# Which hidden pairs stay in plain f32, where VectorE adds up an accumulator, and at which steps the side jobs of the next batch start, in a fused attention and feed-forward kernel

## The chip, the cores and the metric

The kernel runs on one core of one Trainium2 chip. The metric is the device time of one execution in microseconds. Before the change it was 2100.04 us, the median of three runs (2099.92 to 2102.28). The profiled execution took 2101.02 us, and its span, from the first instruction to the last, is 2099.2 us.

## The reference

Four batches of 12480 tokens with 128 channels go through an attention with 49 agents and then through a feed-forward layer with 2048 hidden units. Everything is f32.

```python
a2k = sm(agents, k)            # softmax over the 12480 keys, scaled by 1/sqrt(128)
agent_v = a2k @ v              # 49 x 128 per batch
q2a = sm(q, agents)            # softmax over the 49 agents
x = (q2a @ agent_v).reshape(49920, 128)
h = x @ w_in                   # 49920 x 2048
g = h - np.tanh(h)
return g @ w_out
```

## The kernel before

The kernel never builds `x`. For each batch it multiplies the 49 agent values by `w_in` once (`project`), so that a hidden value is the product of a token's 49 softmax weights with a 49 x 2048 matrix, kept as a high part `awh` and a low part `awl` in float32r.

The main loop (`fast`, line 820 on) goes over 100 blocks of up to 500 tokens. A block has 8 steps, and a step works on one pair of hidden chunks, 2 x 128 hidden units. Two blocks make a **round** of 16 steps; `pos`, 0 to 15, is the step's place in the round. The text numbers steps by this position. There are 50 rounds. In one step:

- TensorE does the first layer of the step two ahead (`m1`, line 559): six float32r matmuls into a two-bank PSUM buffer `h`.
- ScalarE makes `y = tanh(h)` (line 569) and `z`, a scaled square of `y` (line 574). The cubic law `h - tanh(h)` is near `h * z` for small values.
- VectorE makes the product `g = h * z` (line 579), which also frees the buffer `h`.
- For a **split pair** GpSimd rounds `g` to float32r, the high part `gh` (line 609), and VectorE subtracts it, which gives the low part `gl` (line 614), one step later and behind the next product. TensorE then does the second layer (`m2`, line 628) with twelve float32r matmuls: high part by low and high weights, low part by high weights.
- For a **plain pair** there is no `gh` and no `gl`. TensorE multiplies `g` itself in f32 (`acc<-g,wo_f`). The table `PLAIN` on line 61 names the positions of plain pairs; the first block of all is plain throughout.

The second layer of step k-1 stands on TensorE in step k, behind the first layer of step k+2. It adds up over 8 steps in a two-bank accumulator `acc`. PSUM holds four such two-bank buffers in all, for `h`, `acc`, the transposes `pt` and the side jobs' `misc`. When a block is done, ScalarE copies the first bank out (`take`, line 640) and VectorE adds the second bank to it (`add_up`, line 637), which frees the accumulator. That is at positions 2 and 10, two steps into the next block.

Each round also makes the softmax weights of the next round's tokens: 64 small matmuls (line 504) at about position 4, five short VectorE instructions (lines 517 to 523) between the products of positions 8 and 9, and two transposes at 11 and 15. Beside the first three batches run the side jobs for the next batch (`phase1`): 13 score jobs, the maximum, 13 value jobs (`av`: a subtraction on GpSimd, line 342; an exponential on ScalarE, line 346; 8 matmuls, line 354; an addition to an SBUF sum on VectorE, line 366), the sum and four projection parts (`project`). The tables `KS`, `VS`, `OS` on lines 72 to 75 say at which positions how many jobs of each kind start, and `VGAPS` how many steps a value job rests before its exponential and before its matmuls. A round holds three score jobs, or three value jobs, or neither.

The order of all instructions on each engine is the order in which this Python code issues them (`issue_order`). In a step: the product, then the copy-out and addition of a finished accumulator, then the running side jobs, then tanh and square of the next step, the first layer, the low part, the second layer, and last the starts of new side jobs.

Of the kernel before, what the change touches and what calls it, by code (L numbers as in the profile page):

```python
# [57 lines left out]
LATE = 3  # L58
KV = 3
VB = 4  # L60
PLAIN = (1, 3, 5, 7, 9, 13)
NB = dict(y=2, z=2, g=4, gh=3, gl=3)
Q0 = 2
NV = 10
# [5 lines left out]
T0 = 11  # L70
T1 = 15
KS = {2: 1, 12: 2}
VS = {5: 1, 9: 1, 13: 1}
VGAPS = {5: (6, 2), 9: (3, 1), 13: (4, 2)}
OS = {2: 1, 10: 1}


def width(n):
# [23 lines left out]
class Build:  # L102
# [116 lines left out]
    def phase1(self, b):  # L219
        nc = self.nc  # L220
        st = {}
        kb, vb = (K0 if b == 0 else KV), VB
# [27 lines left out]
        def ahead(kind, load, g, depth):  # L250
            have = st.setdefault(kind, [])
            while len(have) < min(NG, g + depth):
                have.append(load(len(have)))
            return have[g]
# [77 lines left out]
            st["mb_at"] = self.last_name()  # L332

        def av(g, gaps=(0, 1)):
            vt = ahead("v", load_v, g, vb - 1) if b else None
            n = tiles(g)
            sv = st["s"][:, g * GT * A : (g * GT + n) * A].rearrange("p (t a) -> p t a", a=A)
            e3 = sv
            flat = e3.rearrange("p t a -> p (t a)")
            top = st["mb"][:, None, :].broadcast_to([128, n, A])  # L340
            first = self.count()
            (nc.gpsimd if b else nc.vector).tensor_tensor(e3, sv, top, ALU.subtract)
            if b:
                self.wait_for(first, self.mul_at)
            yield from (None,) * (gaps[0] if b else 1)
            nc.scalar.activation(e3, e3, AF.Exp, scale=SCALE)
            yield from (None,) * gaps[1]
            if b:
                ps = self.misc()
                for t in range(n):  # L350
                    r = rows(g, t)
                    odd = t % 2
                    w = A if odd else HALF
                    nc.tensor.matmul(  # L354
                        ps[HALF * odd : HALF * odd + w, : C + 1],
                        flat[:r, t * A : t * A + w],
                        vt[:r, t, : C + 1],
                        start=t < 2,
                        stop=t >= n - 2,
                    )  # L360
                yield
                acc = st["acc"][: HALF + A]
                if g == 0:
                    nc.vector.tensor_copy(acc, ps[: HALF + A, : C + 1])
                else:
                    nc.vector.tensor_tensor(acc, acc, ps[: HALF + A, : C + 1], ALU.add)
                return
            vt = ahead("v", load_v, g, 1)
            if g == 0:
                ph = self.banks("h")  # L370
                st["ps"], st["pr"] = ph[:, 0, :], ph[:, 1, :A]
            ps = st["ps"]
            for t in range(n):
                r = rows(g, t)
                odd = t % 2
                w = A if odd else HALF
                nc.tensor.matmul(
                    ps[HALF * odd : HALF * odd + w, :C],
                    flat[:r, t * A : t * A + w],
                    vt[:r, t, :C],  # L380
                    start=(g == 0 and t < 2),
                    stop=(g == NG - 1 and t >= n - 2),
                )
            yield
            if g == NG - 1:
                em = st["em"]
                for i, (rhs, r) in enumerate(((em, 128), (e3[:, 0, :], 128), (e3[:, 1, :], TAIL))):
                    nc.tensor.matmul(st["pr"], self.ones[:r, :], rhs[:r], start=(i == 0), stop=(i == 2))
                return
            if g in (0, 1):  # L390
                return
            if g in (2, 3):
                st["es", g % 2] = self.work.tile([128, GT * A], F32, tag="es", name="es", bufs=2)
            es = st["es", g % 2]
            e0 = st["s"][:, (g - 2) * GT * A : (g - 1) * GT * A] if g in (2, 3) else es
            nc.vector.tensor_tensor(es, e0, flat, ALU.add)
            if g == NG - 2:
                es = st["es", 0]
                nc.vector.tensor_tensor(es, es, st["es", 1], ALU.add)
                st["em"] = self.small.tile([128, A], F32, tag="m", name="es")  # L400
                nc.vector.tensor_reduce(
                    st["em"], es.rearrange("p (t a) -> p a t", a=A), axis=AX.X, op=ALU.add
                )

        def sums():
            yield
            yield
            if b:
                yield
                yield  # L410
                yield
            if b == 0:
                an, n = st["acc"], HALF + A
                nc.vector.tensor_copy(an[:n, :C], st["ps"][:n, :C])
                pt = self.misc()
                nc.tensor.matmul(pt[:, :A], an[:n, :C], self.sel[:n], start=True, stop=True)
                sm = self.small.tile([128, A], F32, tag="mb", name="mb")
                nc.vector.tensor_scalar(sm, st["pr"], EPS, None, ALU.add)
                nc.vector.reciprocal(sm, sm)
                yield  # L420
                nc.vector.tensor_tensor(self.avs[:, b, :], pt[:, :A], sm, ALU.mult)
                return
            n = HALF + A
            acc = st["acc"][:n]
            pt = self.misc()
            nc.tensor.matmul(pt[:, :A], acc[:, :C], self.sel[:n], start=True, stop=True)
            rows_of = acc[:, C : C + 1].broadcast_to([n, 128])
            nc.tensor.matmul(pt[:, A:A2], rows_of, self.sel[:n], start=True, stop=True)
            yield
            sm = self.small.tile([128, A], F32, tag="sm", name="sm")  # L430
            nc.vector.tensor_scalar(sm, pt[:, A:A2], EPS, None, ALU.add)
            nc.vector.reciprocal(sm, sm)
            nc.vector.tensor_tensor(self.avs[:, b, :], pt[:, :A], sm, ALU.mult)
# [247 lines left out]
    def fast(self):  # L681
# [104 lines left out]
        kq = []  # L786
# [59 lines left out]
        for k, (n, i) in enumerate(steps):  # L846
            b = blocks[n][0]
            pos = (n % 2) * HP + i
            p = n // 2
            if n % NBLK == 0 and i == 0 and b + 1 < B:  # L850
                kq = self.phase1(b + 1)
            begin = kq[0][0].get(pos, 0) if kq and n else 0
            product(k)
            if done and done[0][1] < k - 1:
                self.take(out_at(done[0][0]), acc[done[0][0]])
                finish(done.pop(0)[0])
            if n == LATE and i < NP:
                self.bound(0, i, slice(PCUT[i], PCUT[i + 1]))
            if n == 0 and i in (2, 4):
                run(rest0.pop(0))  # L860
            if n == 0 and i == 5:
                live.append(q1)
            if p + 1 < npair and pos in (T0, T1):
                live.append(t_job(2 * p + 2 + (pos == T1)))
            nxt = []
            self.share(True)
            for gen in live:
                try:
                    next(gen)
                    nxt.append(gen)  # L870
                except StopIteration:
                    pass
            live[:] = nxt
            self.share(False)
            tanhs(k + 1)
            squares(k + 1)
            first_product(k + AHEAD)
            low(1)
            mark = self.last_on(ET.DVE)
            if n == 0:  # L880
                if i == 0:
                    run(rest0.pop(0))
                if i % 2 == 0 and i < HP - 2:
                    go(dec[i // 2 + 1], 3)
                elif i < HP - 2:
                    run(dec[i // 2 + 1])
            if pos in SPLIT and n < 2:
                first = self.count()
                self.split_w_out(SPLIT.index(pos))
                self.hold(first, mark, (ET.Activation, ET.Pool))  # L890
            out(k)
            if p and p + 1 < npair:
                if pos == QL:
                    qt[p + 1] = self.q_load(q_src(p + 1))
                if pos == QS:
                    start(q_job(p + 1))
                    live.insert(0, live.pop())
            for kind in [x[0] for x in kq[:begin]]:
                if kq[0][0] is kind:
                    start(kq.pop(0)[1](pos))  # L900
        low(0)
        out(len(steps))
# [67 lines left out]
```

## Time and profile before

| | |
|---|---|
| median of three runs | 2100.04 us |
| profiled execution, and its span | 2101.02 us, 2099.2 us |
| first product on VectorE, last product | 59.14 us, 2086.47 us |
| granted TensorE clock | 0.995 |
| DMA | 62 GB/s mean |
| mean of one product, one low part (VectorE, 128x1000) | 1195 ns, 1199 ns |
| mean of one high part (GpSimd, 128x1000) | 1344 ns |
| mean of tanh, of square (ScalarE, 128x1000) | 1004 ns, 1040 ns |

A matmul's end is modelled, and matmuls overlap, so TensorE's pace is read from the starts of its instructions. Two matmuls on the two halves of the rows run side by side. A VectorE or ScalarE instruction begins a little before the record of the one ahead ends, so what one costs on its engine is the distance of two starts, not the recorded length. A wait is put down to the semaphore that came last.

### The profile page before, as it was taken

Reading aid. Unit: us, or ns where it says so; the run is one execution under the profiler, and the core shown is the slowest. Engines: PE = TensorE matmul, PEld = TensorE weight load, DVE = VectorE, ACT = ScalarE, POOL = GpSimd, SP = SyncE. Lnnn points to the kernel's source line nnn. Section 1 sums busy time; section 2 is a strip of 40 time slices with the busy share of each in tenths; the row PEclk is TensorE's granted clock in tenths of the full one; section 3 lists DMA queues with packets and bytes.
Section 4 is the critical chain, followed back from the end, with each engine's and each line's share of the span. In section 5 each row is a group of like instructions: output and inputs, shape, how many; then the busy total and the mean of one; then the engine's idle time right before and its main releaser. Section 6 shows DMA issues by size and latency. Waiting matters only on the chain.

```text
span 2099.2 us, 49173 instructions
## 1 busy us (share of the span) xinstructions
PE 2018.4 (96%) x20583; PEld 1462.5 (70%) x20583; DVE 1787.3 (85%) x1937; ACT 1811.7 (86%) x2052; POOL 838.0 (40%) x653
## 2 busy tenths in 40 slices
PE   8899999999999999999999999999999999999998
PEld 7467677766667767776667776767666777767766
DVE  7898888788888888788888889888888888888887
ACT  3888888888898988888888888888888999999987
POOL 1233344443333335543343343455333434334343
PEclk9999999999999999999999999999999999999999
DMA  9322122211112221221012111211100110101100
GB/s 347 120 66 87 51 62 72 71 58 44 50 59 65 73 68 58 81 65 58 28 36 88 59 55 43 67 59 54 49 31 32 42 37 33 52 28 36 38 20 28
DMA packets 76600, 129.68 MB, mean 62 GB/s; under 512 B 5384, under 2 KB 55376, under 8 KB 76368
## 3 DMA queue, kind: packets, MB, share of 16 engines
q1 hardware_dynamic: 76368, 126.44, 18.4%
q8 instruction: 164, 2.69, 0.5%
q14 instruction: 68, 0.56, 0.1%
HBM read 81.10 MB, written 25.56 MB: 51 GB/s over the span
## 4 chain that ended last, share of the span: by engine, by line
PE 46%; DVE 26%; ACT 21%; issue 6%; DMA 1%; POOL 0%; DVEq 0%; SPq 0%; POOLq 0%
PE acc L628 22%; PE h L559 15%; DVE g L579 12%; ACT z L574 10%; ACT y L569 9%; DVE gl L614 8%; PE misc L504 2%; PE misc L354 2%; DVE qs L518 2%; PE pt L534 1%; DVE qe L520 1%; PE misc L300 1%; PE h L272 1%; DVE qs L517 1%; PE misc L466 1%
## 5 line engine op out<-in xcount | busy, mean ns | idle before, releaser
L579 DVE TENSOR_TENSOR g<-h,z 128x1000 f32<-128x1000 f32 (+1 forms) x800 | 955.0, 1194 | 268.8 <-ACT z L574 266.8
L609 POOL TENSOR_SCALAR gh<-g 128x1000 fp32r<-128x1000 f32 (+1 forms) x496 | 665.9, 1342 | 1093.0 <-DVE g L579 1091.9
L569 ACT ACTIVATE y<-h 128x1000 f32<-128x1000 f32 (+1 forms) x800 | 802.2, 1003 | 148.6 <-PE h L559 147.9
L574 ACT ACTIVATE z<-y 128x1000 f32<-128x1000 f32 (+1 forms) x800 | 831.1, 1039 | 25.5
L614 DVE TENSOR_TENSOR gl<-g,gh 128x1000 fp32r<-128x1000 f32 (+1 forms) x496 | 593.5, 1197 | 0.9 <-POOL gh L609 0.9
L559 PE MATMUL h<-pT,awh 49*128 49x504 f32 x1600 | 591.0, 445 | 0.0
L628 PE MATMUL acc<-g,wo_f 64*128 64x500 f32 (+1 forms) x2368 | 548.3, 578 | 0.0
L559 PE MATMUL h<-pT,awl 49*128 49x504 f32 x800 | 403.6, 504 | 37.5 <-DVE g L579 30.0
L628 PE MATMUL acc<-gh,wo_l 64*128 64x500 f32 (+1 forms) x1984 | 403.6, 392 | 22.1 <-POOL pp L525 21.0
L628 PE MATMUL acc<-gh,wo_h 64*128 64x500 f32 (+1 forms) x1984 | 399.3, 386 | 0.0
L628 PEld LDWEIGHTS acc<-g,wo_f 64*128 64x128 f32 x2368 | 237.2, 185 | 148.2 <-issue 127.8
L559 PE MATMUL h<-pb,awh 49*128 49x504 f32 x1600 | 323.1, 388 | 0.0
L628 PE MATMUL acc<-gl,wo_h 64*128 64x500 f32 (+1 forms) x1984 | 316.7, 392 | 1.4 <-DVE gl L614 1.4
L559 PE MATMUL h<-pb,awl 49*128 49x504 f32 x800 | 309.5, 387 | 0.0
L559 PEld LDWEIGHTS h<-pT,awh 49*128 49x128 f32 x1600 | 275.1, 187 | 40.1 <-issue 30.1
L628 PEld LDWEIGHTS acc<-gh,wo_l 64*128 64x128 f32 x1984 | 198.4, 184 | 70.8 <-POOL pp L525 40.2
L559 PEld LDWEIGHTS h<-pT,awl 49*128 49x128 f32 x800 | 148.3, 185 | 119.4 <-DVE g L579 83.3
L628 PEld LDWEIGHTS acc<-gl,wo_h 64*128 64x128 f32 x1984 | 191.7, 185 | 42.9 <-DVE gl L614 16.5
L628 PEld LDWEIGHTS acc<-gh,wo_h 64*128 64x128 f32 x1984 | 201.1, 186 | 28.7
L559 PEld LDWEIGHTS h<-pb,awh 49*128 49x128 f32 x1600 | 159.2, 185 | 27.6
L559 PEld LDWEIGHTS h<-pb,awl 49*128 49x128 f32 x800 | 149.8, 187 | 30.8 <-issue 24.9
L534 PE MATMUL pt<-identr,pp 64*113 64x64 f32 x800 | 86.3, 336 | 1.2 <-POOL pp L525 1.2
(113 smaller groups left out, 1153.6 us busy)
## 6 DMA issues: line engine op xcount, KB each, us to landing
kt<-kT SPq DMA_DIRECT2D x48, 512.0 KB
qt<-qT SPq DMA_DIRECT2D x46, 500.0 KB
outT<-o SPq DMA_DIRECT2D x46, 500.0 KB
pb<-pT SPq DMA_DIRECT2D x200, 96.5 KB
v<-v SPq DMA_DIRECT2D x36, 512.0 KB
vt<-v SPq DMA_DIRECT2D x12, 512.0 KB
raw<-w_in SPq DMA_DIRECT2D x4, 512.0 KB
v<-w_out SPq DMA_DIRECT2D x4, 512.0 KB
```

Of the source, the lines that this page charges most:

```text
L272: nc.tensor.matmul(ps[:, t // 4, (t % 4) * A2 : (t % 4 + 1) * A2], kt[:, t, :], self.ag[:, 0:2, :], start=True, stop=True,)
L354: nc.tensor.matmul(ps[HALF * odd : HALF * odd + w, : C + 1], flat[:r, t * A : t * A + w], vt[:r, t, : C + 1], start=t < 2, stop=t >= n - 2,)
L504: nc.tensor.matmul(to, qt[:, token : token + QUART], self.ag[:, b, :], start=True, stop=True)
L518: nc.vector.tensor_scalar(s, s, EPS, None, ALU.add)
L534: nc.tensor.matmul(ps[:PW, r, t * HALF : (t + 1) * HALF], pp[rows, half * BT + t, :], self.identr[rows, rows], start=True, stop=True,)
L559: nc.tensor.matmul(h[:, c, : BT * TT], aw[a][rows[c], sl], pT[p][rows[c], :], start=k == 0, stop=k == 2)
L569: self.nc.scalar.activation(self.pair(y), h, AF.Tanh, scale=TSC)
L574: self.nc.scalar.activation(z, y, AF.Square, scale=GSC)
L579: self.nc.vector.tensor_tensor(self.pair(g), h, self.pair(z), ALU.mult)
L609: self.nc.gpsimd.tensor_scalar(gh, g, 1.0, 0.0, ALU.mult, ALU.add)
L614: self.nc.vector.tensor_tensor(gl, g, gh.bitcast(F32), ALU.subtract)
L628: nc.tensor.matmul(acc[:, r, :w], weights(c)[rows], g[rows, c * w : (c + 1) * w], start=i == 0 and k == 0, stop=i == NCH // 2 - 1 and k == ...
```

## The change

The diff, cut to its core; line numbers in the changed file are one or two lower from `av` on.

```diff
-PLAIN = (1, 3, 5, 7, 9, 13)
+PLAIN = (1, 3, 7, 8, 9)
...
-VS = {5: 1, 9: 1, 13: 1}
-VGAPS = {5: (6, 2), 9: (3, 1), 13: (4, 2)}
-OS = {2: 1, 10: 1}
+VS = {8: 2, 9: 1}
+VGAPS = {8: (3, 2), 9: (8, 2)}
+OS = {2: 1, 4: 1}
...
         def av(g, gaps=(0, 1)):
-            vt = ahead("v", load_v, g, vb - 1) if b else None
...
             yield from (None,) * (gaps[0] if b else 1)
+            vt = ahead("v", load_v, g, vb - 1) if b else None
             nc.scalar.activation(e3, e3, AF.Exp, scale=SCALE)
...
             if b:
-                yield
-                yield
                 yield
...
-            product(k)
             if done and done[0][1] < k - 1:
                 self.take(out_at(done[0][0]), acc[done[0][0]])
                 finish(done.pop(0)[0])
+            product(k)
...
             for kind in [x[0] for x in kq[:begin]]:
-                if kq[0][0] is kind:
+                if kind is kq[0][0] and kind.get(pos):
                     start(kq.pop(0)[1](pos))
```

The plain pairs are now at 1, 3, 7, 8 and 9: those of 5 and 13 become split, that of 8 becomes plain. The addition of a finished accumulator stands ahead of the step's product on VectorE. Two value jobs start at 8 and one at 9. The maximum, the sum and the projection parts start at 2 and 4, not at 2 and 10, and only there (before, such a job could start at 12 right behind the last score job). The sum rests two steps less, and a block of `v` is loaded when a value job reaches its exponential.

On VectorE, from the low part of position 6 to the low part of position 10, in a round without side jobs, there stood before (`qs`, `qe`, `pp` are the token softmax, `o` the output tile):

```order
L614 TENSOR_TENSOR gl<-g,gh 128x1000
L579 TENSOR_TENSOR g<-h,z 128x1000
L517 TENSOR_REDUCE qs<-qe 128x8
L518 TENSOR_SCALAR qs<-qs 128x8
L519 RECIPROCAL qs<-qs 128x8
L520 TENSOR_TENSOR qe<-qe,qs 128x392
L523 CAST pp<-qe 128x8x49
L579 TENSOR_TENSOR g<-h,z 128x1000
L614 TENSOR_TENSOR gl<-g,gh 128x1000
L579 TENSOR_TENSOR g<-h,z 128x1000
L637 TENSOR_TENSOR o<-o,acc 128x500
L579 TENSOR_TENSOR g<-h,z 128x1000
```

and now:

```order
L612 TENSOR_TENSOR gl<-g,gh 128x1000
L577 TENSOR_TENSOR g<-h,z 128x1000
L515 TENSOR_REDUCE qs<-qe 128x8
L516 TENSOR_SCALAR qs<-qs 128x8
L517 RECIPROCAL qs<-qs 128x8
L518 TENSOR_TENSOR qe<-qe,qs 128x392
L521 CAST pp<-qe 128x8x49
L577 TENSOR_TENSOR g<-h,z 128x1000
L635 TENSOR_TENSOR o<-o,acc 128x500
L577 TENSOR_TENSOR g<-h,z 128x1000 x2
```

The low part of 8 is gone, and the addition stands behind the product of 9 instead of that of 10.

From the product of position 14 to that of position 3 of the next round VectorE had, before (the pair of 13 is plain, so there is no low part between the products of 14 and 15):

```order
L579 TENSOR_TENSOR g<-h,z 128x1000 x2
L614 TENSOR_TENSOR gl<-g,gh 128x1000
L579 TENSOR_TENSOR g<-h,z 128x1000
L614 TENSOR_TENSOR gl<-g,gh 128x1000
L579 TENSOR_TENSOR g<-h,z 128x1000
L614 TENSOR_TENSOR gl<-g,gh 128x1000
L579 TENSOR_TENSOR g<-h,z 128x1000
L637 TENSOR_TENSOR o<-o,acc 128x500
L579 TENSOR_TENSOR g<-h,z 128x1000
```

and now:

```order
L577 TENSOR_TENSOR g<-h,z 128x1000
L612 TENSOR_TENSOR gl<-g,gh 128x1000
L577 TENSOR_TENSOR g<-h,z 128x1000
L612 TENSOR_TENSOR gl<-g,gh 128x1000
L577 TENSOR_TENSOR g<-h,z 128x1000
L612 TENSOR_TENSOR gl<-g,gh 128x1000
L577 TENSOR_TENSOR g<-h,z 128x1000
L612 TENSOR_TENSOR gl<-g,gh 128x1000
L635 TENSOR_TENSOR o<-o,acc 128x500
L577 TENSOR_TENSOR g<-h,z 128x1000 x2
```

A low part stands between every two products from 11 to 1, and one behind the product of 1, and the addition stands ahead of the product of 2.

On GpSimd, in a round with value jobs, there stood before (`s<-s,mb` is a value job's subtraction, `pp` and `qe` the token softmax):

```order
L513 TENSOR_TENSOR qe<-qe,qm 128x392
L342 TENSOR_TENSOR s<-s,mb 128x392
L609 TENSOR_SCALAR gh<-g 128x1000 x2
L525 TENSOR_TENSOR pp<-qe,pp 128x8x49
L342 TENSOR_TENSOR s<-s,mb 128x392
L609 TENSOR_SCALAR gh<-g 128x1000 x3
L342 TENSOR_TENSOR s<-s,mb 128x392
L609 TENSOR_SCALAR gh<-g 128x1000 x5
```

and now:

```order
L511 TENSOR_TENSOR qe<-qe,qm 128x392
L607 TENSOR_SCALAR gh<-g 128x1000 x2
L523 TENSOR_TENSOR pp<-qe,pp 128x8x49
L341 TENSOR_TENSOR s<-s,mb 128x392 x3
L607 TENSOR_SCALAR gh<-g 128x1000 x9
```

The three subtractions stand together, behind `pp` and ahead of the high part of 10.

## The prediction

> **What bounds the kernel now.** The page's first part comes first, for which engine is near full:
>
> ```profile
> PE 2018.4 (96%) x20583; PEld 1462.5 (70%) x20583; DVE 1787.3 (85%) x1937; ACT 1811.7 (86%) x2052; POOL 838.0 (40%) x653
> ```
>
> TensorE shows 96%, but its ends are modelled, so the share doesn't prove it. TensorE's own timeline settles it, here in a round without side jobs, with a split pair and then a plain one:
>
> ```profile
> 1798.80 0.40 PE L628 MATMUL acc<-gh,wo_l 64*128 64x500 f32 x2
> ...
> 1800.17 0.39 PE L559 MATMUL h<-pT,awh 49*128 49x504 f32 x1
> ...
> 1800.85 1.85 PE L628 MATMUL acc<-g,wo_f 64*128 64x500 f32 x8
> ...
> 1803.22 0.41 PE L628 MATMUL acc<-gh,wo_l 64*128 64x500 f32 x2
> ```
>
> From one second layer to the next nothing is idle. A split step costs TensorE 1800.85 - 1798.80 = 2.05 us, a plain one 1803.22 - 1800.85 = 2.37. The windows by round say whether this sums up (the columns after the length are the busy times of PE, PEld, DVE, ACT, POOL):
>
> ```profile
> 1784.10:1822.60 38.50, 37.53 (x347) 27.46 (x346) 33.41 (x35) 35.11 (x39) 15.43 (x13) 1.00 0.12 38
> 1139.00:1179.90 40.90, 39.93 (x538) 29.14 (x538) 35.94 (x39) 36.37 (x42) 15.43 (x13) 1.00 0.22 75
> 1342.10:1383.80 41.70, 40.56 (x394) 29.01 (x394) 34.21 (x38) 35.89 (x42) 20.89 (x16) 1.00 0.24 74
> ```
>
> They are a round without side jobs, one with three score jobs and one with three value jobs. In the first, ten split and six plain steps make 10 x 2.05 + 6 x 2.37 = 34.7 of 38.5 us; the rest is the token softmax's matmuls and waits. The three score jobs add 2.4 us and the value jobs 3.2, as work for TensorE does. So TensorE sets the pace, except where it waits. The waits lie at the change of blocks. First position 9, from VectorE's timeline and that of all engines:
>
> ```profile
> 1796.71 1.20 DVE L579 TENSOR_TENSOR g<-h,z 128x1000 f32<-128x1000 f32 x1 [1.60 <-ACT z L574]
> ...
> 1798.93 1.19 DVE L579 TENSOR_TENSOR g<-h,z 128x1000 f32<-128x1000 f32 x1
> 1801.14 1.20 DVE L579 TENSOR_TENSOR g<-h,z 128x1000 f32<-128x1000 f32 x1 [1.02 <-ACT z L574]
> ```
> ```profile
> 1803.37 1.19 DVE L579 TENSOR_TENSOR g<-h,z 128x1000 f32<-128x1000 f32 x1
> ...
> 1804.48 0.55 DVE L517 TENSOR_REDUCE qs<-qe 128x8 f32<-128x392 f32 x1
> ...
> 1805.27 1.86 PE L628 MATMUL acc<-g,wo_f 64*128 64x500 f32 x8
> ...
> 1806.92 1.19 DVE L579 TENSOR_TENSOR g<-h,z 128x1000 f32<-128x1000 f32 x1
> ...
> 1807.48 0.56 ACT L640 COPY o<-acc 128x500 f32<-128x500 f32 x1
> ...
> 1808.03 1.19 DVE L614 TENSOR_TENSOR gl<-g,gh 128x1000 fp32r<-128x1000 f32 x1
> 1808.26 0.49 PE L628 MATMUL acc<-gh,wo_l 64*128 64x500 f32 x2 [0.44 <-POOL pp L525]
> ...
> 1810.25 0.67 DVE L637 TENSOR_TENSOR o<-o,acc 128x500 f32<-128x500 f32 x1
> 1810.39 0.49 PE L559 MATMUL h<-pT,awl 49*128 49x504 f32 x1 [0.38 <-DVE g L579]
> ...
> 1810.83 1.19 DVE L579 TENSOR_TENSOR g<-h,z 128x1000 f32<-128x1000 f32 x1
> ...
> 1811.18 0.59 PE L628 MATMUL acc<-g,wo_f 64*128 64x500 f32 x2
> ```
>
> The second layer of 7 starts at 1805.27 and that of 8 at 1808.26: 2.99 us where 2.37 would do. The page names GpSimd's `pp`, but the new accumulator takes the buffer that the product of 9 frees, and that ended at 1806.92 + 1.19 = 1808.11. From there to the second layer of 9 are 2.92 us, not 2.05: the first layer at 1810.39 waits for the product of 10 to free a buffer, with the old accumulator not yet added up. At position 2 the same, smaller:
>
> ```profile
> 1788.48 0.43 PE L628 MATMUL acc<-gh,wo_l 64*128 64x500 f32 x2
> ...
> 1790.06 0.67 DVE L637 TENSOR_TENSOR o<-o,acc 128x500 f32<-128x500 f32 x1
> ...
> 1790.20 0.50 PE L559 MATMUL h<-pT,awl 49*128 49x504 f32 x1
> ...
> 1791.00 1.00 PE L628 MATMUL acc<-g,wo_f 64*128 64x500 f32 x4
> ```
>
> 1791.00 - 1788.48 = 2.52, so 0.47 lost. VectorE's cost for a product or a low part is 1804.48 - 1803.37 = 1.11 us, less than the recorded 1.19.
>
> **The change, part by part.** I reckon in the times of this round.
>
> *Plain pairs.* One fewer in each of 49 rounds. The pair of 13 lies where TensorE doesn't wait: 2.37 - 2.05 = 0.32 us saved. The pair of 5 lies ahead of the wait at 9, whose end VectorE sets by its run from the product of 5 at 1796.71. The new low part of 5 goes into the idle time ahead of the product of 7: 1798.93 + 2 x 1.11 = 1801.15, and that product began at 1801.14. So the product of 9 stays where it was, and 0.32 us saved by 5 only lengthen the wait. VectorE has 1.11 us more per round, 54 us in all, and its cover is this row, its time of waiting for ScalarE:
>
> ```profile
> L579 DVE TENSOR_TENSOR g<-h,z 128x1000 f32<-128x1000 f32 (+1 forms) x800 | 955.0, 1194 | 268.8 <-ACT z L574 266.8
> ```
>
> *Addition first, position 10.* With the low part of 8 gone, the addition starts where that stood, 1808.03 (the copy ended at 1807.48 + 0.56 = 1808.04), and frees the old accumulator at 1808.7. The changed program gives that buffer to the next first layer. The second layer of 8, now plain, runs from 1808.26 as before, and that of 9 follows after 2.37 without a wait: 1810.63 instead of 1811.18, 0.55 saved.
>
> *Addition first, position 2.* It saves the 0.47 if the addition is done in time. The first layer that waits for it stood at 1790.20, in the next round, 38.49 later, at 1828.69. With 0.55 and 0.32 saved and its own 0.35 of waiting gone, TensorE gets there at 1827.47. VectorE now has a low part behind every product from 10 on, 2.22 us a step against TensorE's 2.05. In the rows of
>
> ```profile
> 1784.12 1.19 DVE L579 TENSOR_TENSOR g<-h,z 128x1000 f32<-128x1000 f32 x1
> ...
> 1816.28 1.20 DVE L579 TENSOR_TENSOR g<-h,z 128x1000 f32<-128x1000 f32 x1 [0.48 <-ACT z L574]
> ...
> 1822.61 1.19 DVE L579 TENSOR_TENSOR g<-h,z 128x1000 f32<-128x1000 f32 x1
> ```
>
> the round's length is 1822.61 - 1784.12 = 38.49, and the product of 13 waited for `z`. TensorE is 0.55 earlier and the tanh of 12 no longer sits behind a late first layer, so I estimate it 0.7 earlier, at 1815.6. From it stand five products and five low parts ahead of the addition: 1815.6 + 10 x 1.11 = 1826.7, done 0.67 later at 1827.4. That is 0.1 us in time, a narrow cover; each us of lateness would cost that us. I take the 0.47, and 0.1 per round, 5 us, for the narrowness.
>
> The sum is 0.32 + 0.55 + 0.47 = 1.34 us per round, 49 x 1.34 = 65.7. The new round would be some 37.1 us. The waits of TensorE for products, which this draws on, are there in every kind of round:
>
> ```profile
> PEld h L559 <- DVE g L579: 83.3, 119, 2.1
> PE h L559 <- DVE g L579: 30.0, 70, 1.7
> ```
>
> *Value jobs.* Three subtractions now stand on GpSimd between `pp` and the high part of 10, in 12 rounds. Durations on GpSimd, in a round with value jobs, and the group of a like instruction:
>
> ```profile
> 1366.24 1.03 POOL L525 TENSOR_TENSOR pp<-qe,pp 128x392 fp32r<-128x392 f32 x1 [1.35 <-DVE pp L523]
> 1367.34 1.85 POOL L342 TENSOR_TENSOR s<-s,mb 128x392 f32<-128x392 f32 x1
> 1369.64 1.03 POOL L609 TENSOR_SCALAR gh<-g 128x1000 fp32r<-128x1000 f32 x1 [0.45 <-DVE g L579]
> 1371.33 1.84 POOL L609 TENSOR_SCALAR gh<-g 128x1000 fp32r<-128x1000 f32 x1 [0.66 <-DVE g L579]
> ```
> ```profile
> L513 POOL TENSOR_TENSOR qe<-qe,qm 128x392 f32<-128x392 f32 x50 | 42.5, 849 | 40.0 <-DVE qm L511 40.0
> ```
>
> A high part takes 1.03 us, or 1.84 beside a low part. The subtraction's 1.85 was always beside one; alone it lies between 0.85 (same size) and 1.85. In its new place no low part runs, so I take 1.03, nearest to `pp`. [...] In the times of the quiet round, `pp` ends at 1808.1, three subtractions at 1811.2, the high part of 10 at 1812.3. TensorE needs it at 1810.63 + 2.37 and a transpose, past 1813: hidden. The exponentials, matmuls and additions are as many as before. The `v` loads leave SP's queue later, but two jobs ahead, about eight steps; I cost them at nothing, and a late one at the step it delays.
>
> *Maximum, sum, projection.* Two projection parts per round now start at 2 and 4, and their VectorE instructions fall into the run from the product of 5 to that of 9, which sets the wait at 9:
>
> ```profile
> L480 DVE TENSOR_REDUCE mx<-awh 49x1 f32<-49x512 f32 x15 | 10.0, 667 | 0.0
> L472 DVE TENSOR_TENSOR awl<-misc,awh 113x512 fp32r<-113x512 f32 x14 | 9.6, 683 | 2.9 <-ACT awh L469 2.9
> ```
>
> That is 2 x 1.35 = 2.7 us in six rounds, of which one part of two was near there before and TensorE's own matmuls cover some: between nothing and 2.7, I take 1 us each, 6 us. The maximum's two parts now nearly touch, the sum starts sooner; for these I take zero, 5 us either way.
>
> Against the profiled execution's 2101.0 us: 2101.0 - 65.7 + 5 + 6 = 2046.3, say **2046 us**. The median of the runs was 1 us lower, which is within what can be told: a measurement here tells some 0.2% (4 us) from no change.
>
> **The rivals.**
>
> *VectorE's pace eats the gain at 2.* Place: positions 11 to 1, seven low parts in a row. If the addition comes 0.5 us later than reckoned, 49 x 0.5 = 25 us go back: 2071. For it: 2.22 against 2.05 a step, and a cover of 0.1. Against: the first product of the stretch begins earlier, and side jobs of TensorE in it widen the cover.
>
> *GpSimd holds the high part of 10.* If a subtraction takes 1.85 alone too, three end at 1813.7 and the high part at 1814.7: TensorE waits 1.3, then for the low part and the next product, 2.5 in all, in 12 rounds 30 us: 2076. For it: every one of them took 1.85. Against: the low part beside each.
>
> *Slower: VectorE is the bound.* If its waits for `z` stay as they are because ScalarE's chain and VectorE's, not TensorE, set the round, the added low part comes on top: 49 x 1.11 = 54 us, 2155. This decides if VectorE's unbroken run is longer than TensorE's. For it: VectorE 85%, ScalarE 86%, TensorE's weight loads 70%. Against: the starts on TensorE touch outside of the named waits. [...]
>
> *The change doesn't free the buffer at 2.* If the first layer there still waits for the product, that now stands behind the addition: it starts at 1827.4 and ends at 1828.6, and the first layer stays at 1828.69. The other savings would be swallowed there, and the round would keep its length: 2101, no change. For it: this is what it waited for before. Against: the changed program gives it the accumulator's buffer.
>
> **How the numbers follow.** Forecast 0.69; VectorE's pace 0.12; GpSimd 0.08; no change 0.04; slower 0.07. Faster is 0.69 + 0.12 + 0.08 = 0.89, same 0.04, slower 0.07. The range: at the best the 5 and 6 us aren't lost and the maximum brings 5: 2101 - 65.7 - 5 = 2030; at the other end the two milder rivals, 2076 and a little: 2078. Outside lie 0.11 and some misses.
>
> **What would show it.** Right: a round without side jobs of 37.1 to 37.3 us; TensorE's first layer waiting for line 635 or nothing at 2 and 10, not for a product; a wait of about 0.9 at 9 still there; subtractions behind `pp` of about 1.03 us. Wrong: rounds of over 38 us with TensorE waiting for low parts in 11 to 1; subtractions of 1.85; VectorE without idle time.

## The result and the profile after

The changed kernel takes 2046.62 us (median of four runs, 2046.16 to 2047.11) against 2100.12 for the kernel before: a ratio of 0.9743, 95% interval 0.9726 to 0.976. The forecast was 2046. The profiled execution took 2046.16, its span is 2044.4. The page's first part:

```profile
PE 1994.1 (98%) x20779; PEld 1458.3 (71%) x20779; DVE 1835.7 (90%) x1986; ACT 1806.2 (88%) x2052; POOL 978.3 (48%) x702
```

TensorE is busy 24 us less in a span that is 55 us shorter: by these shares, whose ends are modelled, more than half of the gain is waiting that has gone. VectorE is busy 48 us and GpSimd 140 us longer, in a shorter span. The windows of three rounds, a round without side jobs (a *quiet* round below), one with three score jobs and one with three value jobs:

```profile
1737.90:1775.10 37.20, 37.07 (x350) 27.13 (x350) 33.98 (x36) 34.97 (x39) 19.61 (x14) 1.00 0.12 39
1149.00:1188.50 39.50, 39.37 (x544) 29.10 (x542) 36.46 (x39) 36.18 (x42) 18.76 (x14) 1.00 0.23 78
1307.60:1348.50 40.90, 40.15 (x398) 29.62 (x396) 36.33 (x39) 35.86 (x42) 20.62 (x17) 1.00 0.25 75
```

The quiet round is 1.3 us shorter, the score round 1.4, the value round only 0.8. Measured from product to product at position 0, the quiet round went from 38.46 to 37.21. How the waits at the change of blocks look now, first from the product of 5 to the second layer of 9, in the timeline:

```profile
1750.18 1.20 DVE L577 TENSOR_TENSOR g<-h,z 128x1000 f32<-128x1000 f32 x1 [1.37 <-ACT z L572]
...
1757.94 0.55 DVE L515 TENSOR_REDUCE qs<-qe 128x8 f32<-128x392 f32 x1
1758.43 1.85 PE L626 MATMUL acc<-g,wo_f 64*128 64x500 f32 x8
1758.53 0.17 DVE L516 TENSOR_SCALAR qs<-qs 128x8 f32<-128x8 f32 x1
...
1759.85 1.19 DVE L577 TENSOR_TENSOR g<-h,z 128x1000 f32<-128x1000 f32 x1
...
1761.09 0.30 PEld L626 LDWEIGHTS acc<-g,wo_f 64*128 64x128 f32 x4 [0.55 <-DVE g L577]
1761.10 1.95 PE L626 MATMUL acc<-g,wo_f 64*128 64x500 f32 x8
1761.22 0.68 DVE L635 TENSOR_TENSOR o<-o,acc 128x500 f32<-128x500 f32 x1 [0.17 <-ACT o L638]
...
1763.56 1.43 PE L626 MATMUL acc<-g,wo_f 64*128 64x500 f32 x6
```

The second layer of 8 still waits for the product of 9, now 0.55 us by the weight load. The wait at 10 is gone: 1763.56 - 1761.10 = 2.46 us, where there were 2.92. But the second layers of 7 and 8 are closer as well, 1761.10 - 1758.43 = 2.67 instead of 2.99, because VectorE gets from the product of 5 to that of 9 in 9.67 us where it took 10.21. The prediction said that this run would not change. In it stands one instruction of another length, `qs` on 128x8, 0.17 us here. The groups by line, of before and then of the changed kernel (the last numbers are the sum and the mean of one in ns):

```profile
L518 DVE TENSOR_SCALAR qs<-qs 128x8 f32<-128x8 f32 x50 | 33.9, 678 | 1.7
```
```profile
L516 DVE TENSOR_SCALAR qs<-qs 128x8 f32<-128x8 f32 x50 | 8.6, 171 | 1.7
```

Half a microsecond a round, on the mean of 50, has gone from an instruction that the diff does not touch. In the kernel before, the high part of 8 ran on GpSimd at that moment, as its timeline shows:

```profile
1804.72 1.03 POOL L609 TENSOR_SCALAR gh<-g 128x1000 fp32r<-128x1000 f32 x1 [3.40 <-DVE g L579]
1805.06 0.71 DVE L518 TENSOR_SCALAR qs<-qs 128x8 f32<-128x8 f32 x1
```

The small instruction ends at 1805.77, the high part at 1805.75. Pair 8 is plain now and has no high part. At position 2, in the timeline of the changed kernel:

```profile
1742.36 0.56 ACT L638 COPY o<-acc 128x500 f32<-128x500 f32 x1
1742.95 0.68 DVE L635 TENSOR_TENSOR o<-o,acc 128x500 f32<-128x500 f32 x1 [0.30 <-ACT o L638]
1743.68 0.18 PEld L557 LDWEIGHTS h<-pT,awl 49*128 49x128 f32 x1 [0.36 <-DVE o L635]
```

The first layer waits for the addition, as the change intends, and not for the product; the addition in turn waits 0.30 us for the copy-out. From the second layer of 9 to that of 1 there were 18.29 us before (1811.18 to 1829.47) and are 18.09 now (1763.56 to 1781.65): 0.20 less, where the prediction had counted 0.79 (0.32 and 0.47). From 7 to 9 it is 5.13 instead of 5.91, 0.78 less. The remaining 0.27 of the round's 1.25 lie between 1 and 7, where the pair of 5 is now split: from its second layer to that of 6 it is 2.05 us instead of 2.37.

### The profile page after: what moved, and what is told of

Same layout as the page of the kernel before. It is cut to its first block, busy times and chain, and to the rows that moved or that the text cites. A ratio compares the mean times of both kernels' runs of the same rounds, so it can differ in the third digit from the quotient of the medians.

```text
span 2044.4 us, 49580 instructions
## 1 busy us (share of the span) xinstructions
PE 1994.1 (98%) x20779; PEld 1458.3 (71%) x20779; DVE 1835.7 (90%) x1986; ACT 1806.2 (88%) x2052; POOL 978.3 (48%) x702
## 4 chain that ended last, share of the span: by engine, by line
PE 55%; DVE 28%; ACT 10%; issue 5%; DMA 1%; POOL 1%; DVEq 0%; SPq 0%; POOLq 0%
PE acc L626 31%; PE h L557 17%; DVE g L577 11%; DVE gl L612 9%; ACT z L572 4%; ACT y L567 4%; PE misc L354 2%; PE misc L502 2%; DVE qe L518 1%; PE misc L300 1%; DMA v<-v 1%; PE h L272 1%; PE pt L532 1%; DVE qs L515 1%; POOL gh L607 1%
## 5 line engine op out<-in xcount | busy, mean ns | idle before, releaser
L607 POOL TENSOR_SCALAR gh<-g 128x1000 fp32r<-128x1000 f32 (+1 forms) x545 | 843.7, 1549 | 735.7 <-DVE g L577 690.3
L612 DVE TENSOR_TENSOR gl<-g,gh 128x1000 fp32r<-128x1000 f32 (+1 forms) x545 | 667.5, 1225 | 6.9 <-POOL gh L607 6.2
L626 PE MATMUL acc<-g,wo_f 64*128 64x500 f32 (+1 forms) x1976 | 460.8, 583 | 11.9 <-DVE g L577 7.2
L626 PE MATMUL acc<-gh,wo_l 64*128 64x500 f32 (+1 forms) x2180 | 432.8, 387 | 0.3 <-POOL gh L607 0.2
L626 PE MATMUL acc<-gh,wo_h 64*128 64x500 f32 (+1 forms) x2180 | 432.8, 387 | 0.0
L626 PE MATMUL acc<-gl,wo_h 64*128 64x500 f32 (+1 forms) x2180 | 340.5, 386 | 1.3 <-DVE gl L612 0.8
L626 PEld LDWEIGHTS acc<-g,wo_f 64*128 64x128 f32 x1976 | 188.6, 186 | 156.8 <-issue 109.7
L626 PEld LDWEIGHTS acc<-gh,wo_h 64*128 64x128 f32 x2180 | 214.9, 186 | 38.2
L626 PEld LDWEIGHTS acc<-gl,wo_h 64*128 64x128 f32 x2180 | 210.7, 185 | 41.1 <-DVE gl L612 4.8
L523 POOL TENSOR_TENSOR pp<-qe,pp 128x392 fp32r<-128x392 f32 x50 | 51.8, 1037 | 245.7 <-DVE pp L521 237.7
```

Of the source, the lines that this page charges most:

```text
L523: nc.gpsimd.tensor_tensor(pp[:, :, HALF:PW], ev, pp[:, :, :A].bitcast(F32), ALU.subtract)
L607: self.nc.gpsimd.tensor_scalar(gh, g, 1.0, 0.0, ALU.mult, ALU.add)
L612: self.nc.vector.tensor_tensor(gl, g, gh.bitcast(F32), ALU.subtract)
L626: nc.tensor.matmul(acc[:, r, :w], weights(c)[rows], g[rows, c * w : (c + 1) * w], start=i == 0 and k == 0, stop=i == NCH // 2 - 1 and k == ...
```

## The experiments

Theory: the gain is made at 8 and 9, by the high part that no longer holds up `qs`; little comes from the addition's place, since VectorE's pace between 10 and 2 takes back what is given at 2. Rival: the prediction's own sum, in which the addition's place gives 0.55 and 0.47. Ratios are to runs of the kernel before on the same chip. Round lengths (us) are distances of the products at position 0, medians for quiet and value rounds; rounds are counted from 0. Rounds 4 and 5 hold the maximum, 9 to 12 the last value job, the sum and the projection. The times of two rows can't be compared to the microsecond: the kernel before took 2100.12 to 2102.67 us on the chips used, and the first product comes between 59.1 and 62.7 us in the profiled executions. So what a kernel gains or loses as a whole is also read from its 49 rounds.

| kernel | time, us | ratio to before, 95% interval | quiet | value | 4 and 5 | 9 to 12 |
|---|---|---|---|---|---|---|
| before | 2100.12 | 1 | 38.46 | 41.78 | 83.4 | 164.4 |
| changed | 2046.62 | 0.9743 (0.9726 to 0.976) | 37.21 | 40.93 | 79.1 | 160.6 |
| before, new plain pairs | 2071.11 | 0.9859 (0.9842 to 0.9875) | 37.33 | 41.05 | 82.6 | 163.6 |
| before, addition first | 2070.07 | 0.9856 (0.9839 to 0.9872) | 37.73 | 41.18 | 80.7 | 161.6 |
| before, new side jobs | 2112.53 | 1.0054 (1.0037 to 1.007) | 38.46 | 42.64 | 82.5 | 165.3 |
| before, 8 plain for 5 | 2064.48 | 0.9823 (0.9806 to 0.9839) | 37.41 | 41.36 | 80.7 | 163.6 |
| changed, unread high part of 8 | 2075.36 | 0.9875 (0.9858 to 0.9891) | 37.73 | 41.46 | 80.2 | 162.6 |
| changed, 13 plain too | 2049.23 | 0.9754 (0.9738 to 0.9771) | 37.16 | 41.00 | 79.7 | 160.9 |
| changed, old side jobs | 2065.30 | 0.982 (0.9804 to 0.9837) | 37.19 | 40.98 | 82.2 | 164.6 |
| changed, old places, new value jobs | 2067.01 | 0.9827 (0.981 to 0.9843) | 37.20 | 40.94 | 82.3 | 164.8 |
| changed, 13 plain for 3 | 2059.40 | 0.9798 (0.9781 to 0.9814) | 37.46 | 41.01 | 80.5 | 161.1 |
| changed, addition last | 2053.13 | 0.9765 (0.9749 to 0.9782) | 37.32 | 41.00 | 79.4 | 160.9 |
| changed, 14 plain for 3 | 2062.72 | 0.9811 (0.9794 to 0.9827) | 37.64 | 40.93 | 80.5 | 161.1 |
| changed, no low part of 13 | 2037.40 | 0.9691 (0.9675 to 0.9707) | 36.87 | 40.94 | 79.1 | 159.7 |

**The three parts one by one.** First the list of plain pairs alone, in the kernel before:

```diff
-PLAIN = (1, 3, 5, 7, 9, 13)
+PLAIN = (1, 3, 7, 8, 9)
```

> The kernel before with only the new table of plain pairs (1, 3, 7, 8, 9). The prediction's sum: the wait for the accumulator at 9 ends where it did, the first layer behind it waits no longer, 0.55 us a round, and 0.32 for the pair of 13, less a little because the product at position 2 still stands ahead of the addition: about 0.75 us a round, 2064 us. The new theory, that the high part of 8 on GpSimd held up the small VectorE instruction of the token softmax (0.71 us before, 0.17 after), adds 0.55 at 9, but the seven low parts in a row take it back at 2: round about 37.7 us, 2063 us. The totals agree; the trace tells them apart: the small instruction at 0.17 us and a second layer of 7 to that of 8 of 2.7 us (new theory), or 0.7 and about 3.3 us (the prediction).

Then the addition ahead of the product alone:

```diff
-            product(k)
             if done and done[0][1] < k - 1:
                 ...
+            product(k)
```

> The kernel before with only the addition put ahead of the product. Both theories: at position 10 the first layer then waits for the second layer ahead of it and not for the product, 0.5 us less, and at 2 the 0.47 us go in full, since the plain pair of 13 still gives VectorE time: about 0.95 us a round, 2054 us. The rival, that the addition frees nothing in time: 2100 us.

And the side jobs alone (`VS`, `VGAPS`, `OS`, the rule of beginning, the sum's rest and the load of `v`, with the old list and the product first):

> The kernel before with only the changes to the side jobs (value jobs at 8 and 9, maximum, sum and projection at 2 and 4, the load at the exponential, the start rule). The prediction: 6 us slower by the projection parts in VectorE's run ahead of position 9, 2106 us. The reading of the trace after: value rounds gained 0.45 us less than quiet ones, 12 times, and the four rounds of sum and projection 0.3 less, so that the side jobs cost about 9 us: 2109 us. The rival, that three subtractions together spare low parts and high parts from each other: 2090 us.

The list alone takes 1.13 us off the quiet round, the addition alone 0.73, both together 1.25: they are not additive. In the trace of the list alone the small instruction takes 172 ns and the second layers of 7 and 8 lie 2.67 us apart, as the new theory said; the whole took 2071 us, 7 and 8 more than the two sums, since rounds 4, 5 and 9 to 12 gained little (82.6 and 163.6). The wait at 10 that the addition's place removes is gone already where pair 8 has no low part: from the second layer of 8 to that of 9 it is 2.47 us with the list alone and 2.46 with both. The addition alone fell short of the 0.95 that the theory gave it, and took 2070 us where 2054 were expected. From the second layer of 8 to that of 10 it takes 0.52 off (5.68 to 5.16), as expected, but from that of 0 to that of 1 only 0.25 (2.52 to 2.27) and not 0.47. The side jobs alone make the kernel slower, by 0.86 us in each value round, more than expected (2112.53 us for 2106 to 2109). In its timeline, at positions 8 to 11 of a value round, the rival that was named for GpSimd is to be seen at work:

```profile
383.53 1.19 DVE L612 TENSOR_TENSOR gl<-g,gh 128x1000 fp32r<-128x1000 f32 x1
383.58 3.80 POOL L341 TENSOR_TENSOR s<-s,mb 128x392 f32<-128x392 f32 x3
...
386.33 1.19 DVE L577 TENSOR_TENSOR g<-h,z 128x1000 f32<-128x1000 f32 x1
...
387.34 2.02 POOL L607 TENSOR_SCALAR gh<-g 128x1000 fp32r<-128x1000 f32 x2
...
388.40 2.00 DVE L612 TENSOR_TENSOR gl<-g,gh 128x1000 fp32r<-128x1000 f32 x1 [0.88 <-POOL gh L607]
```

Pair 8 is still split here. One of the three subtractions runs beside its low part, the three take 3.80 us, the high part of 10 comes late, and the low part waits 0.88 for it and then takes 2.00 beside the high part of 11. The groups of the subtraction in the kernel before, in this one and in the changed one (mean of one, in ns):

```profile
L342 POOL TENSOR_TENSOR s<-s,mb 128x392 f32<-128x392 f32 (+1 forms) x39 | 70.3, 1802 | 43.0 <-DVE g L579 37.9 <-DVE mb L331 4.2
```
```profile
L341 POOL TENSOR_TENSOR s<-s,mb 128x392 f32<-128x392 f32 (+1 forms) x39 | 49.6, 1298 | 0.0
```
```profile
L341 POOL TENSOR_TENSOR s<-s,mb 128x392 f32<-128x392 f32 (+1 forms) x39 | 34.5, 913 | 0.0
```

The new places of the value jobs need the new list: only without the low part of 8 do all three run alone. With the new list, however, the subtractions are short in their old places as well, 915 ns on the mean in the changed kernel with all side jobs as before.

**Is it the high part of 8?** Only 5 and 8 exchanged, in the kernel before:

```diff
-PLAIN = (1, 3, 5, 7, 9, 13)
+PLAIN = (1, 3, 7, 8, 9, 13)
```

> The kernel before with the pair of 5 split and that of 8 plain, 13 still plain (1, 3, 7, 8, 9, 13), so as many plain pairs as before. The prediction's sum: 0.55 us a round because the low part of 8 is gone from ahead of the product of 10, 2074 us. The new theory: the high part of 8 is gone from beside the token softmax as well, so another 0.55: 1.1 us a round, 2047 us.

And the changed kernel with a high part of pair 8 that GpSimd makes and nobody reads:

```diff
             gh = None if plain else self.high(g)
+            if n >= 2 and n % 2 * HP + i == 8:
+                self.high(g)
```

> The changed kernel with one high part more, of the plain pair of 8, on GpSimd, which nothing reads. The new theory: it starts beside the token softmax again, the small VectorE instruction takes about 0.7 us and not 0.17, the product of 9 and the second layer of 8 come 0.54 later in each of 49 rounds: 2046.6 + 26 = 2073 us. The rival, that 0.71 us was that instruction's own and the gain at 9 came from elsewhere: no change, 2047 us, since nobody waits for this high part.

The exchange gives 1.05 in the quiet round, as this theory has it, and the small instruction takes 172 ns. The whole gains less than expected (2064 us for 2047), since value rounds follow by 0.42 only and rounds 9 to 12 by 0.8 in four. The unread high part costs 0.52 us a round, and the small instruction is long again in the kernel with it, though it waits for nothing that GpSimd makes:

```profile
L516 DVE TENSOR_SCALAR qs<-qs 128x8 f32<-128x8 f32 x50 | 34.0, 679 | 1.7
```

In the trace of the kernel before, a high part that had begun 0.35 us earlier (once 0.66) was under way in 48 of the 50 cases, and each time the small instruction ended 0.02 to 0.03 us behind it; the two cases without a high part took 170 and 171 ns. What makes the one wait for the other no run here shows.

**What pair 13 and the addition's place are worth beside the rest.** The changed kernel with pair 13 plain as well, and the changed kernel with the product ahead of the addition again:

```diff
-PLAIN = (1, 3, 7, 8, 9)
+PLAIN = (1, 3, 7, 8, 9, 13)
```

> The changed kernel with the pair of 13 plain again: 1, 3, 7, 8, 9, 13. If the seven low parts in a row set the pace from 11 to 2, where the trace after lost 0.6 us a round against the reckoning, VectorE gets 1.11 us of room there, TensorE pays 0.32, and the round is 0.3 us shorter: 2046.6 - 15 = 2032 us. If that loss is of another cause, TensorE's 0.32 us come on top: 2062 us.

```diff
+            product(k)
             if done and done[0][1] < k - 1:
                 ...
-            product(k)
```

> The changed kernel with the product again ahead of the addition of the accumulator, as in the kernel before; everything else stays. By the prediction's own working the addition's place was worth 0.47 a round at 2 and 0.55 at 10, of which the step at 10 is by now also cured by the plain pair 8: quiet round 37.21 + 0.47 = 37.7, the whole 2070. By the reading of the runs so far (0.73 alone, but 37.33 against 37.19 beside the new list of plain pairs, so 0.13 here): quiet round 37.33, the whole 2052 to 2055.

Neither case of the first came: 37.16 against 37.21, so splitting 13 gains nothing, though by the prediction's 2.37 and 2.05 TensorE works 0.32 us less there. The second hit: the addition's place is worth 0.11 in the quiet round and about 6 us in all, against the 0.55 + 0.47 of the prediction. With the addition last it is still 2.47 us from the second layer of 8 to that of 9, so the addition's place is worth nothing at 10 here, and the 0.11 lie at 2.

**VectorE's pace.** Two lists that relieve VectorE between 10 and 2 at no cost in plain pairs:

```diff
-PLAIN = (1, 3, 7, 8, 9)
+PLAIN = (1, 7, 8, 9, 13)
```

> The changed kernel with pair 13 plain and pair 3 split: PLAIN = (1, 7, 8, 9, 13). Theory, VectorE's pace: from 11 over the end of the round to 1 VectorE goes through split pairs at 2.22 a step, and that is what ate the gain at 2; one low part less in this run gives it 1.11 of slack, and TensorE has as many matmuls as before, so that the quiet round goes from 37.21 to 36.8 to 36.9 and the whole to 2028 to 2034. Rival: the steps from 1 to 5 have no slack either, and a low part at 3 (1.1) moves the products of 4 and 5 back; then the quiet round is 37.2 to 38.0 and the whole 2047 to 2085.

```diff
-PLAIN = (1, 3, 7, 8, 9)
+PLAIN = (1, 7, 8, 9, 14)
```

> As the run with pair 13 plain and 3 split, but with 14 plain: PLAIN = (1, 7, 8, 9, 14). Theory, VectorE's pace: the run of split pairs that VectorE goes through without rest is then 10 to 13 and 15 to 0; the quiet round goes below 37.0 as with 13, and the nearer the relief lies to position 2 the more of it is left there: 36.7 to 36.9, the whole 2025 to 2032. Rival, the split pair 3 costs what is gained: 37.2 to 38.0, the whole 2047 to 2085.

Both came out as the rival said, 0.25 and 0.43 longer. They don't settle whether VectorE holds TensorE up between 10 and 2, because they also put a low part at 3. The next run relieves VectorE without touching the work of TensorE or GpSimd; its kernel leaves one low part out of the result:

```diff
-                r2.append((n, i, g, None) if gh is None else (n, i, gh, self.low(g, gh)))
+                r2.append(
+                    (n, i, g, None)
+                    if gh is None
+                    else (n, i, gh, gh if n % 2 * HP + i == 13 else self.low(g, gh))
+                )
```

> The changed kernel with the low part of pair 13 left out: its four matmuls of the low part read the high part once more, so that TensorE has the same matmuls in the same order, GpSimd the same work, and VectorE one subtraction of 1.11 us less in each round, in the run of split pairs from 10 to 0 (the low part of that pair is missing from the result). Both runs that relieved this stretch before gave TensorE or VectorE other work as well. Theory, VectorE's pace takes back what the addition's place gives at 2 (waits of 0.27, 0.18 and 0.20 of TensorE between 15 and 2): the quiet round goes from 37.21 to 36.6 to 36.9, the whole to 2018 to 2032. Rival, TensorE itself sets the time from 10 to 2 and its waits there are only of its own making: the quiet round stays at 37.1 to 37.2, the whole at 2042 to 2048.

The quiet round falls to 36.87, inside what VectorE's pace was to give. Its window and what is left at 2:

```profile
1844.40:1881.30 36.90, 36.76 (x352) 27.12 (x350) 33.06 (x36) 34.89 (x39) 18.86 (x14) 1.00 0.12 40
```
```profile
1849.21 0.68 DVE L635 TENSOR_TENSOR o<-o,acc 128x500 f32<-128x500 f32 x1 [0.23 <-ACT o L638]
...
1849.94 0.18 PEld L557 LDWEIGHTS h<-pT,awl 49*128 49x128 f32 x1 [0.38 <-DVE o L635]
```

So the pace costs at least 0.34 us in a quiet round: from the second layer of 13 to that of 14 it is 2.46 us instead of 2.63, and on to that of 15 it is 2.07 instead of 2.23. That is as much as splitting 13 was to save on TensorE (0.32). The first layer at 2 waits as long as ever, because the addition waits for ScalarE's copy-out. The whole gained 9.2 us, less than the 15 to 29 expected: value rounds and rounds 4 and 5 are as long as before, score rounds 0.2 shorter. In value rounds the pace is not what ends last.

**The side jobs' places.** The changed kernel with all side jobs as before, and with the new value jobs, but the old places for the maximum, the sum and the projection:

```diff
-OS = {2: 1, 4: 1}
+OS = {2: 1, 10: 1}
...
+                yield
+                yield
+                yield
+                yield
...
-                if kind is kq[0][0] and kind.get(pos):
+                if kq[0][0] is kind:
```

> The changed kernel with the side jobs of before: new table of plain pairs and addition first only. The prediction had them cost about 6 us by the projection: 2040 us without. The trace after says 5 us for the value rounds and 4 us for sum and projection: 2037 us. The rival, that the new places of the subtractions are worth something beside the new low parts, since a subtraction beside a low part took 1.85 us and alone 0.96: slower, 2055 us or more.

> The changed kernel with its value jobs kept (two begun at 8, one at 9), but the maximum, the sum and the projection put back to where the kernel before has them: places 2 and 10, the old rule of beginning, and the sum resting four steps longer so that it still comes after the last value addition. With all the old side jobs the changed kernel took 2065.30, with the new ones 2046.62: 18.7 us. Theory, places: the gain comes from where the maximum, the sum and the projections stand; then rounds 4 and 5 take about 82.2 together and rounds 9 to 12 about 164.6, as with all the old jobs, the long waits of TensorE at the starts of rounds 5 and 10 are back, and the whole is 2062 to 2067. Rival, grouping: the gain comes from the value jobs standing together at 8 and 9; then rounds 9 to 12 stay near 160.6, rounds 4 and 5 near 79.1, and the whole is 2045 to 2049.

The second settles it: 82.3 and 164.8 as with all the old jobs, and value rounds of 40.94 in either. Beside the new list the value jobs' grouping is worth nothing and the places 17 to 18 us by the sums of the 49 rounds (the times, 2065.30 and 2067.01 against 2046.62, differ by 19 and 20, the ratios by 16 and 18). What the old places cost, at the start of round 5 in the timeline of the second kernel:

```profile
268.68 0.31 PE L317 MATMUL misc<-ident,m 128*49 128x128 f32 x1
269.14 0.58 PE L536 MATMUL pt<-identr,pp 64*113 64x64 f32 x8
271.36 0.49 PE L561 MATMUL h<-pT,awl 49*128 49x504 f32 x1 [1.63 <-DVE g L581]
```

The maximum's matmul stands directly ahead of the transposes of 15, and the next first layer waits 1.63 us for a product. That the two take the last free buffers is my reading of the code, not a run's result. The windows behind it (the third number from the end is the granted clock):

```profile
271.50:272.50 1.00, 1.00 (x10) 0.85 (x12) 0.97 (x2) 0.15 (x1) 1.00 (x1) 1.00 0.30 97
...
273.50:274.50 1.00, 1.00 (x8) 0.82 (x6) 0.18 (x2) 0.93 (x1) 0.00 (x0) 0.50 0.02 8
274.50:275.50 1.00, 1.00 (x8) 0.85 (x6) 1.00 (x1) 0.05 (x1) 0.00 (x0) 0.50 0.00 0
```

About 1.6 us after the wait's end TensorE's granted clock falls to 0.50 for 3.41 us. What that costs is seen at round 10, which took 45.60 us with a wait of 1.11 us and a fall behind it, and round 22, which took 44.23 with a wait of 1.12 and no fall: 1.4 us. After round 0 this kernel has five waits of over 1 us (1.11 to 1.63, 6.6 in all), and the clock fell after four of them. Waits and falls together make some 12 of the 18 us at most; the rest is not traced. The changed kernel has no wait of over 1 us after round 0, and no fall from there to its last product. But the length of a wait does not settle it. In the traces of all 14 kernels, from round 1 to the last product, the clock fell after each of six waits of 1.63 us, after five of 23 from 1.04 to 1.23, and, in the kernel with only 5 and 8 exchanged, after two of 0.81. What decides among these no run here shows.

## Why the prediction was right

**The total and the quiet round were right, their parts were not.** The prediction took 1.34 us per round and 5 us off for the narrowness, 1.24 in effect. Measured were 1.25, of other terms: where it had 0 ahead of 9, 0.55 at 10 and 0.69 from there to 2, the traces have about 0.6, 0.46 and 0.20. That the sums agree is luck.

- *Exchange of 5 and 8: 0 predicted at the wait at 9, and what the missing low part gives at 10.* This step failed. "So the product of 9 stays where it was" rested on VectorE's run from 5 to 9 keeping its length. It was 0.54 us shorter, since `qs` is no longer held up by the high part of 8; the row that shows it, 0.71 us for 128x8, stands in the timeline of before, between two rows that the prediction quotes. With it the 0.32 us that splitting 5 saves on TensorE count as well, which the prediction let the wait swallow. The exchange alone is worth 1.05.
- *Addition first at 10: 0.55.* Right as a wait (2.92 became 2.46), wrong as a term of its own: the missing low part of 8 does it all, since it is 2.47 with the addition last too. The whole quiet round is then only 0.11 longer.
- *Addition first at 2: 0.47 less 0.1; splitting 13: 0.32.* Of these 0.7 us little came: 0.20 from the second layer of 9 to that of 1. The rival of VectorE's pace, given 0.12, is true in kind at about two thirds of its price (0.34 a round, not 0.5), which takes back the 0.32 of splitting 13, and the copy-out at 2 holds the addition by another 0.3. The prediction looked at the low parts ahead of the addition, not at the copy-out.
- The predicted sign for the step, the first layers at 2 and 10 waiting for the addition or nothing, was there. The wait of about 0.9 at 9 was 0.55 on the weight load.

**Value jobs: right in their size, not hidden.** The subtraction alone took 0.95 us, the median of the trace (1.03 predicted; the group's mean of 0.91 has three smaller ones in it). But a value round without long waits before gained 0.85 instead of 1.25, 0.4 less. In the timeline of the changed kernel the high parts of 10 and 11 follow without a gap, and the second gets ahead of the low part of 10:

```profile
1331.91 2.80 POOL L341 TENSOR_TENSOR s<-s,mb 128x392 f32<-128x392 f32 x3
...
1334.67 2.02 POOL L607 TENSOR_SCALAR gh<-g 128x1000 fp32r<-128x1000 f32 x2
...
1335.73 2.00 DVE L612 TENSOR_TENSOR gl<-g,gh 128x1000 fp32r<-128x1000 f32 x1 [0.45 <-POOL gh L607]
...
1337.87 1.20 DVE L577 TENSOR_TENSOR g<-h,z 128x1000 f32<-128x1000 f32 x1
...
1339.12 0.50 PE L557 MATMUL h<-pT,awl 49*128 49x504 f32 x1 [0.37 <-DVE g L577]
```

The low part takes 2.00 us, the next product comes late, and TensorE's first layer waits 0.37 us for it; a quiet round has no such wait there. The rival of GpSimd is thus there in small: not by 1.85 for a subtraction, but by the order in which a high part and a low part begin. It doesn't make the new places worse than the old: with the old value jobs beside the new list this wait is missing, TensorE waits 0.35 us instead at 9 (0.13 in a quiet round), and the value round is 40.98 as well.

**Maximum, sum, projection: 6 us lost, predicted; 17 to 18 gained beside the new list, measured.** The step failed in its sign. It priced the projection's VectorE instructions where they now stand and took the old places for free. With the old places the rounds 4, 5 and 9 to 12 would have kept nearly their old length, 82.2 and 164.6 after 83.4 and 164.4, and hardly any of the gain would have reached them. In the kernel before, the new side jobs changed these rounds by -0.9 and +0.9 only, so the old places cost this much only beside the new list.

**Why the total still fits.** 49 rounds at 1.25 make 61.2 us, and the rounds together gained 55.0, nearly all of the spans' 2099.2 - 2044.4 = 54.8. Of the 6.2 between, 2.6 are the first round's, which is 1.3 longer instead of 1.25 shorter, 3.5 those of rounds 9 to 12 and their like in the other two batches, and 1.6 the twelve value rounds'. Most of these gained 0.8 to 0.9, but round 5 gained 2.7: in the kernel before TensorE waited 1.14 us in it, and its clock fell behind that. The other rounds give 1.5 back. The prediction subtracted 6 for the projection, and that the two agree is chance. The rivals of no change and of a slower kernel didn't come: the first layer at 2 did get the accumulator's buffer, and VectorE, though busy for 90% of the span, still waits for `z` (1.37 us ahead of the product of 5).

## What to carry to other kernels

Before pricing a removed instruction by its own time, look for what it held up on the other engine: compare the same small instruction's duration in places with and without a GpSimd instruction beside it (here 679 and 171 ns). Savings at neighbouring waits don't add up, so try the parts alone and together; a part that loses alone (the side jobs, +11 us) can gain beside the others (here the places of the maximum, the sum and the projection, 17 to 18 us). Places of side jobs that leave TensorE a wait of over 1 us cost the wait and, in 11 of 29 cases here, a stretch at a granted clock of 0.50 behind it.

## What the hardware showed unexpectedly

- A VectorE instruction on 128x8 took 679 ns on the mean where a GpSimd high part had started before it, and 171 ns where none had.
- A VectorE low part that began while a high part ran on GpSimd took 1.45, 1.82 and 2.00 us with 0.41, 0.77 and 0.96 us of the high part left, otherwise 1.19 as recorded. Where the low part began first, it kept its 1.19, and the high part took about 1.84 (the median of 187 in the kernel before) instead of 1.03. In either order it was the one that began second that took longer.
- From round 1 to the last product, stretches of 3.41 us at a granted clock of 0.50 began 0 to 1.6 us behind the end of waits of 0.81 to 1.63 us on TensorE, behind every one of 1.63 and few of the shorter ones. In round 0 of the changed kernel none began behind waits of 1.71 and 1.81 us, so the length of the wait alone does not decide.
